# Four weight conversions in another order, in the first slots of an MLP that follows a spectral mixer

## The chip, the cores and the metric

The kernel runs on one core of one Trainium2 chip. The metric is the device time of one execution in microseconds, lower is better; the time before is 2548.9 us, the median of 3 runs (2548.44 to 2549.2).

## What is computed

Eight sequences of 3072 tokens with 256 channels go through a real Fourier transform along the sequence, a complex 256 x 256 mixing with a soft threshold, the inverse transform, and then a two-layer MLP with softplus:

```
X = rfft(x, axis=1);  Yr = Xr @ w_r - Xi @ w_i + b_r;  Yi = Xr @ w_i + Xi @ w_r + b_i
Y = soft_threshold(Yr, 0.01) + 1j * soft_threshold(Yi, 0.01)
x = irfft(Y).reshape(24576, 256)
h = x @ w_in;  g = max(h, 0) + log1p(exp(-|h|));  out = g @ w_out      # 256 -> 2048 -> 256
```

## The kernel before

**Numbers in two parts.** Every matrix product of the MLP is made of three matmuls (`mm3`, L248 to L251): high part times high part, high times low, low times high. So each weight is kept as a pair of a rounded high part and a low part that holds the rest. The first layer's products are further written as a seven-product scheme (the indices A11 to S4 and B11 to T4), so a first-layer weight tile `w1` holds 7 blocks in 2 parts (128 x 1792 numbers of 4 bytes, 896 KB) and a second-layer tile `w2` holds 128 x 1024 (512 KB).

**Keys and slots.** The MLP's work is a list of keys (batch b, pair of token blocks bp, pair of hidden blocks mp). The first eight keys, called key 0 to key 7 here, use the weights with m2 = 0 to 7 of both layers. Each key takes four slots of the program; key k starts at slot 4k. In a slot, `slot_products` issues 3 or 6 first-layer matmuls (tiles `psc` and `pse`), then come one step of the transform work planned for this slot (such as `s1_four`, eight matmuls), loads planned for it, and last `slot_second` issues 6 second-layer matmuls (tile `pso`). Key k reads its `w2` from its own last slot, 4k + 3, to slot 4k + 6, the third of the next key.

**Where weights come from.** In the first pass over the weights the inputs (64-bit numbers) must first be converted. `split_w` (L183 to L238) does that in pieces, one piece a slot: squares and scalings on ScalarE (ACT) and VectorE (DVE), one product on GpSimd (POOL, L203), sums on DVE (L219 to L231 for `w_in`, one L223 for `w_out`), the rounding to the high part on ACT (L233), the low part on DVE (L235), and a store of both parts to DRAM (L237, `w_dr`). Key 0 to key 7 are converted once; a conversion marked `own` in the table `turns` writes straight into a `w1` or `w2` tile which its key then reads, the others write elsewhere and their key loads the tile back from DRAM in `stream_w` (L245): `w1` four slots before its key starts, `w2` one slot before.

```
    def w2_tile():
        return sb.tile([P, 2 * 2 * D], F32R, tag="w2", name="w2")
...
        if own:
            w = w_t[which, (0, 0, m2)] = w1_tile() if which else w2_tile()
...
            for which, lead in ((1, 4), (0, 1)):
                if i >= NM // 2 or (which, i) not in made:
                    at(4 * i - lead, stream_w, which, i % (NM // 2), key)
```

There are two `w1` buffers and two `w2` buffers (the pool has bufs=2). Tiles get them in the order in which the program asks; a tile that asks while both are taken gets the one whose reader is done first, and its first writer waits for that reader. A conversion asks for its own tile in its third piece, two slots after it starts.

**The table.** A row of `turns` is (layer: 1 for w_in, 0 for w_out; m2; slot at which the conversion starts; slot at which the raw weight is loaded; where the raw weight lies; own or not). Loads and stores nearly all stand in one queue, that of SyncE (SP), in the order in which the program issues them; a DMA whose buffer isn't free holds up all that stand behind it there.

Of the kernel before, what the change touches and what calls it, by code (L numbers as in the profile page):

```python
# [34 lines left out]
def tile_spectral_mixer_mlp(ctx, tc, x, w_r, w_i, bias, bias_0, w_in, w_out, f, f_hi, f_lo, g1, g3, g3_hi, g3_lo, hm, out):  # L35
# [77 lines left out]
    def less(src, hi, lo, eng=None, sign=1.0, what=None):  # L113
# [15 lines left out]
        (0, 2, -21, -27, 'l', 0),  # L129
        (1, 4, -16, -22, 'dp', 0),  # L130
        (1, 0, -11, -17, 'w64', 1),
        (1, 5, 3, -3, 2048, 0),
        (0, 3, 7, -2, 3072, 1),
        (1, 6, 9, 1, 4096, 0),
        (0, 4, 12, 6, 0, 1),
        (0, 5, 16, 10, 1024, 1),
        (0, 6, 20, 11, 'w64', 1),
        (1, 7, 22, 12, 'w64', 1),
# [1019 lines left out]
```

## Time and profile before

| | |
|---|---|
| median of 3 runs | 2548.9 us |
| profiled execution | 2550.98 us |
| its span, first to last instruction | 2549.2 us |
| mean granted clock of TensorE in it | 0.994 |
| busy share of the span: PE, DVE, ACT, POOL | 98%, 63%, 64%, 3% |

The profiled execution is 2.1 us above the median of the runs, so a sum made against it is carried over to the median as a difference. PE is TensorE's matmuls, PEld its weight loads. The times in rows are microseconds from the span's start; the four conversions lie between about 134 us (slot 4) and 180 us.

### The profile page before, as it was taken

To read this page: it belongs to the slowest core of one execution; us is meant where nothing else is said; L and a number is where in the kernel's file an instruction comes from. 1 tells how busy PE (TensorE), PEld (TensorE's weight loads), DVE (VectorE), ACT (ScalarE), POOL (GpSimd) and SP (SyncE) were. 2 spreads that over 40 slices of the span, in tenths; PEclk is the share of its full clock that TensorE was granted. 3 is DMA by queue.
4 is the path that set the end of the run, shared out by engine and by line. 5 is a ranking of instruction groups with operands and counts; after the bars stand their busy time and mean duration, and the time that the engine had idled before them with its cause. 6 is when DMAs were issued, how large, how long until landed. Compare 5 with 4: busy or idle time off the path is not lost.

```text
span 2549.2 us, 46550 instructions
## 1 busy us (share of the span) xinstructions
PE 2509.3 (98%) x18092; PEld 2003.1 (79%) x18092; DVE 1608.9 (63%) x2657; ACT 1633.9 (64%) x3005; POOL 63.7 (3%) x127
## 2 busy tenths in 40 slices
PE   8899999999999999999999999999999999999999
PEld 5667778877787777877788777787778887888887
DVE  4688675675665766657656676466664666655554
ACT  4476566666666666666666666666666666666665
POOL 2310000000000000000000000000000000000000
PEclk9899999999999999999999999999999999999999
DMA  8776666657557576575665666666656556455543
GB/s 238 234 235 199 202 205 174 201 179 234 174 168 230 170 214 187 163 222 187 190 204 175 186 203 186 197 186 203 203 181 193 174 174 207 155 160 183 176 153 116
DMA packets 224920, 485.52 MB, mean 190 GB/s; under 512 B 42028, under 2 KB 134796, under 8 KB 224700
## 3 DMA queue, kind: packets, MB, share of 16 engines
q1 hardware_dynamic: 220244, 478.16, 60.5%
q8 instruction: 143, 2.34, 0.4%
q0 software_dynamic: 2624, 2.32, 0.4%
q10 hardware_dynamic: 1832, 2.07, 0.3%
q14 instruction: 77, 0.63, 0.1%
HBM read 373.36 MB, written 82.71 MB: 179 GB/s over the span
## 4 chain that ended last, share of the span: by engine, by line
PE 93%; DMA 3%; DVE 2%; SPq 1%; issue 1%; ACT 1%; POOL 0%; DVEq 0%; ACTq 0%
PE pso L249 15%; PE pso L250 13%; PE pso L251 13%; PE psc L249 7%; PE psc L251 7%; PE psc L250 7%; PE pse L249 5%; PE pse L250 5%; PE pse L251 5%; PE psf L649 3%; PE psf L251 2%; PE psf L250 2%; PE psf L249 2%; PE psf L339 2%; PE psf L594 2%; PE psf L419 2%
## 5 line engine op out<-in xcount | busy, mean ns | idle before, releaser
L794 DVE TENSOR_TENSOR gl<-t,gh 128x512 fp32r<-128x512 f32 x768 | 531.2, 692 | 295.1 <-ACT gh L788 293.0
L773 ACT COPY t<-psc 128x512 f32<-128x512 f32 x576 | 337.2, 585 | 566.8 <-PE psc L251 566.4
L778 DVE TENSOR_TENSOR t<-pse,t 128x512 f32<-128x512 f32 x576 | 396.6, 689 | 423.1 <-ACT t L773 286.1
L249 PE MATMUL pso<-gh,w 128*128 128x512 f32 x1536 | 619.8, 404 | 0.0
L251 PE MATMUL pso<-gh,w 128*128 128x512 f32 x1536 | 599.8, 390 | 0.0
L250 PE MATMUL pso<-gl,w 128*128 128x512 f32 x1536 | 599.7, 390 | 0.0
L788 ACT CAST gh<-t 128x512 fp32r<-128x512 f32 x768 | 476.8, 621 | 78.9 <-PE pso L251 56.6
L784 ACT ACTIVATE t<-t 128x512 f32<-128x512 f32 x576 | 365.4, 634 | 77.1 <-DVE t L778 76.9
L249 PEld LDWEIGHTS pso<-gh,w 128*128 128x128 f32 x1536 | 288.7, 188 | 127.9 <-issue 72.6
L251 PEld LDWEIGHTS pso<-gh,w 128*128 128x128 f32 x1536 | 288.5, 188 | 62.4
L250 PEld LDWEIGHTS pso<-gl,w 128*128 128x128 f32 x1536 | 289.1, 188 | 50.9
L249 PE MATMUL psc<-y_sb,w 128*128 128x512 f32 x768 | 301.4, 392 | 4.0 <-ACT t L773 3.1
L251 PE MATMUL psc<-y_sb,w 128*128 128x512 f32 x768 | 300.0, 391 | 0.0
L250 PE MATMUL psc<-y_sb,w 128*128 128x512 f32 x768 | 299.6, 390 | 0.0
L249 PE MATMUL pse<-y_sb,w 128*128 128x512 f32 x576 | 227.4, 395 | 2.9 <-DVE t L778 2.4
L250 PE MATMUL pse<-y_sb,w 128*128 128x512 f32 x576 | 225.3, 391 | 0.5 <-DVE y_sb L720 0.5
L251 PE MATMUL pse<-y_sb,w 128*128 128x512 f32 x576 | 224.7, 390 | 0.0
L249 PEld LDWEIGHTS psc<-y_sb,w 128*128 128x128 f32 x768 | 144.6, 188 | 37.9 <-ACT t L773 4.0
L251 PEld LDWEIGHTS psc<-y_sb,w 128*128 128x128 f32 x768 | 144.6, 188 | 31.0
L250 PEld LDWEIGHTS psc<-y_sb,w 128*128 128x128 f32 x768 | 144.5, 188 | 29.9
L251 PE MATMUL psf<-wmh,l 128*128 128x256 f32 x504 | 142.6, 283 | 0.0
L250 PE MATMUL psf<-wml,l 128*128 128x256 f32 x504 | 142.5, 283 | 0.0
(159 smaller groups left out, 2809.9 us busy)
## 6 DMA issues: line engine op xcount, KB each, us to landing
w<-w_dr SPq DMA_DIRECT2D x190, 896.0 KB
w<-w_dr SPq DMA_DIRECT2D x185, 512.0 KB
dp<-d_dr SPq DMA_DIRECT2D x114, 192.0 KB
ap<-a_dr SPq DMA_DIRECT2D x168, 128.0 KB
shrunk<-z SPq DMA_DIRECT2D x336, 64.0 KB
d_dr<-d SPq DMA_DIRECT2D x84, 256.0 KB
x<-in_x SPq DMA_DIRECT2D x105, 192.0 KB
a_dr<-a SPq DMA_DIRECT2D x102, 192.0 KB
```

The lines of the kernel that those rows point to most:

```text
L249: nc.tensor.matmul(ps, wh, xh, start=start, stop=False, skip_group_check=more)
L250: nc.tensor.matmul(ps, wh, xl, start=False, stop=False, skip_group_check=more)
L251: nc.tensor.matmul(ps, wl, xh, start=False, stop=stop, skip_group_check=more)
L339: nc.tensor.matmul(banks[i][64 * odd:64 * odd + 64, :], f2[64 * i:64 * i + 48, 64 * odd:64 * odd + 64], t[64 * i:64 * i + 48], start=True, ...
L419: nc.tensor.matmul(xv[n:n + 64, i, v, g, k], t[rows, 2 * i + g, k * P + n:k * P + n + 64], g1_t[rows, 2 * i + g].rearrange("p (c s) -> p c ...
L594: nc.tensor.matmul(banks[e][cols, c], g3_half[rows, kind], both[j][rows, c], start=True, stop=True)
L649: nc.tensor.matmul(banks[v][j:j + m, at:at + n], d[64 * v:64 * v + rows, n2 % 4, k * P + j:k * P + j + m], h[64 * v:64 * v + rows, n2 % 4, ...
L773: nc.scalar.copy(t, banks[bank])
L778: nc.vector.tensor_tensor(out=t, in0=banks[bank], in1=t, op=ALU.add)
L784: nc.scalar.activation(t, banks[bank] if bank else t, AF.Softplus)
L788: nc.scalar.copy(gh, ct[key, what])
L794: nc.vector.tensor_tensor(out=gl, in0=ct.pop((key, what)), in1=gh.bitcast(F32), op=ALU.subtract)
```

## The change

Four rows of the table are written in another order and at other slots. The conversions for key 3 and key 4 of the second layer (`own`) now start at slots 3 and 10 (before 7 and 12), those for key 5 and key 6 of the first layer, which go through DRAM, at 7 and 13 (before 3 and 9). The slots of their raw loads are exchanged with them; the place of each raw weight stays its own.

```
-        (1, 5, 3, -3, 2048, 0),
-        (0, 3, 7, -2, 3072, 1),
-        (1, 6, 9, 1, 4096, 0),
-        (0, 4, 12, 6, 0, 1),
+        (0, 3, 3, -3, 3072, 1),
+        (1, 5, 7, -2, 2048, 0),
+        (0, 4, 10, 1, 0, 1),
+        (1, 6, 13, 6, 4096, 0),
```

No instruction is added or taken away; all that follows is their order. Two places are shown. The first is SP's queue of DMAs from the load of key 2's `w2` on (slot 7). Here `w2_dr2` to `w2_dr4` and `w1_dr3` to `w1_dr6` are the converted weights of key 2 to key 6 in DRAM, `x0` a piece of the next sequence, `a` a result of the first transform step, `stage` the mixing weights, and the number in a tile's name rises with the order in which tiles are asked for. Before:

```order
L245 DMA w2_1260<-w2_dr2_89 128x1024
L237 DMA w1_dr5_84<-y1_78 128x1792
L1038 DMA g3_half_73<-in_g3_hi 128x128
L245 DMA w1_1301<-w1_dr3_82 128x1792
L104 DMA a_dr_189<-a_1296 96x512
L104 DMA a_dr_189<-a_1298 96x512
L318 DMA x0_95<-in_x 48x2x512 x2
L179 DMA y1_78<-in_w_out 128x2x512
L145 DMA stage_1352<-in_w_r 128x2x256
L145 DMA stage_1354<-in_w_i 128x2x256
L179 DMA w64_1388<-in_w_out 128x2x512
L237 DMA w2_dr3_90<-w2_1323 128x1024
```

And with the change:

```order
L245 DMA w2_1255<-w2_dr2_89 128x1024
L237 DMA w2_dr3_90<-w2_1204 128x1024
L1038 DMA g3_half_73<-in_g3_hi 128x128
L245 DMA w1_1296<-w1_dr3_82 128x1792
L104 DMA a_dr_189<-a_1291 96x512
L104 DMA a_dr_189<-a_1293 96x512
L318 DMA x0_95<-in_x 48x2x512 x2
L179 DMA y1_78<-in_w_out 128x2x512
L145 DMA stage_1349<-in_w_r 128x2x256
L145 DMA stage_1351<-in_w_i 128x2x256
L179 DMA w64_1381<-in_w_out 128x2x512
L237 DMA w1_dr5_84<-y1_78 128x1792
```

The places in the queue are the same; the two stores `w1_dr5` and `w2_dr3` have changed places. In both, the bias (256 KB), the raw `w_in` of key 7 (512 KB) and the load of key 4's `w1` (896 KB) come next. The tile of key 3 (`w2_1323` before, `w2_1204` now) was asked for after that of key 2 (`w2_1260`), and is now asked for ahead of it (`w2_1255`).

The second place is ACT's queue around the rounding of an own tile. Before, in slots 9 to 11, key 3's tile (`t` are results of the first layer taken out of the accumulator `psc`, which the next first-layer product overwrites):

```order
L196 ACTIVATE wu_1326<-y1_78 128x512
L199 ACTIVATE y1_78<-y1_78 128x512
L773 COPY t_1344<-psc_1268 128x512
L233 CAST w2_1323<-y1_78 128x512
L784 ACTIVATE t_1344<-t_1344 128x512
```

With the change, in slots 13 to 15, key 4's tile:

```order
L773 COPY t_1443<-psc_1389 128x512
L233 CAST w2_1408<-y1_78 128x512
L196 ACTIVATE wu_1449<-y1_78 128x512
L199 ACTIVATE y1_78<-y1_78 128x512
L773 COPY t_1465<-psc_1389 128x512
```

The rounding now stands ahead of a copy out of the accumulator, with two instructions of the next conversion between them.

## Rows read from the trace of the kernel before

**Rows 1.** The page, part 1: busy time and share of each engine.

```profile
PE 2509.3 (98%) x18092; PEld 2003.1 (79%) x18092; DVE 1608.9 (63%) x2657; ACT 1633.9 (64%) x3005; POOL 63.7 (3%) x127
```

**Rows 2.** Waits of PE from 260 us on: total us, times, longest.

```profile
PE psf L419 <- issue: 1.3, 2, 0.9
PE psc L249 <- DMA w<-w_dr: 0.9, 1, 0.9
```

**Rows 3.** Timeline of PE, slots 10 to 16: start, us, instruction, [idle before, releaser].

```profile
154.87 0.39 PE L251 MATMUL pso<-gh,w 128*128 128x512 f32 x1
...
156.67 0.40 PE L249 MATMUL pso<-gh,w 128*128 128x512 f32 x1
...
158.05 0.39 PE L249 MATMUL psc<-y_sb,w 128*128 128x512 f32 x1
...
160.46 0.50 PE L249 MATMUL pse<-y_sb,w 128*128 128x512 f32 x1 [1.57 <-DVE t L778]
...
167.61 0.50 PE L249 MATMUL psc<-y_sb,w 128*128 128x512 f32 x1 [0.86 <-ACT t L773]
...
172.69 0.39 PE L249 MATMUL psc<-y_sb,w 128*128 128x512 f32 x1
...
173.99 0.50 PE L249 MATMUL pse<-y_sb,w 128*128 128x512 f32 x1 [0.46 <-DVE t L778]
```

**Rows 4.** Timeline of SP's queue, 140 to 164 us: start and length of issue.

```profile
140.00 0.44 SPq L179 DMA_DIRECT2D y<-in_w_out  x1
143.83 0.35 SPq L245 DMA_DIRECT2D w<-w_dr  x1
147.77 0.34 SPq L237 DMA_DIRECT2D w_dr<-y  x1
...
163.50 0.41 SPq L245 DMA_DIRECT2D w<-w_dr  x1
```

**Rows 5.** Chain of waits from 148 us on: start, us, what.

```profile
163.50 6.50 DMA w<-w_dr
```

**Rows 6.** Windows: us, engines' busy time, PE clock, DMA share, GB/s (last two).

```profile
146.00:146.50 0.50, 0.50 (x4) 0.42 (x3) 0.50 (x2) 0.50 (x2) 0.00 (x0) 1.00 1.02 418
146.50:147.00 0.50, 0.50 (x4) 0.42 (x3) 0.50 (x2) 0.50 (x2) 0.00 (x0) 1.00 0.12 41
148.50:153.00 4.50, 4.50 (x22) 3.46 (x19) 3.70 (x7) 4.44 (x9) 1.23 (x1) 1.00 0.98 324
```

**Rows 7.** DMA traffic from 148 to 170 us.

```profile
DMA packets 2853, 6.89 MB, mean 313 GB/s; under 512 B 259, under 2 KB 899, under 8 KB 2851
...
q1 hardware_dynamic: 2851, 6.87, 95.9%
```

**Rows 8.** Timeline of ACT, slots 9 to 11.

```profile
151.87 0.67 ACT L196 ACTIVATE wu<-y 128x512 f32<-128x512 f32 x1
152.44 0.67 ACT L199 ACTIVATE y<-y 128x512 f32<-128x512 uint32 x1
...
155.30 0.62 ACT L233 CAST w<-y 128x512 fp32r<-128x512 f32 x1 [0.77 <-PE pso L251]
155.85 0.63 ACT L784 ACTIVATE t<-t 128x512 f32<-128x512 f32 x1
```

**Rows 9.** Timeline of PE, three of its waits ahead of 134 us.

```profile
28.64 2.34 PE L393 MATMUL psf<-y,ap 128*128 128x128 f32 x8 [2.55 <-ACT y L307]
...
64.97 1.25 PE L393 MATMUL psf<-y,ap 128*128 128x128 f32 x8 [3.19 <-DMA ap<-a]
...
130.45 0.61 PE L249 MATMUL psc<-y_sb,w 128*128 128x512 f32 x1 [2.25 <-ACT t L773]
```

**Rows 10.** Windows after waits of 2.25 and 1.57 us, as in rows 6.

```profile
130.50:134.00 3.50, 3.50 (x9) 2.74 (x10) 3.44 (x7) 2.67 (x5) 0.00 (x0) 0.53 0.02 5
160.50:164.00 3.50, 3.50 (x18) 2.02 (x19) 3.43 (x11) 2.36 (x4) 0.00 (x0) 1.00 0.90 302
```

**Rows 11.** Timeline of PE, its longest wait after 180 us.

```profile
206.35 1.13 PE L393 MATMUL psf<-ap 128*128 128x128 f32 x8 [1.44 <-issue]
```

## The prediction

> **What bounds the kernel now.** I read the page's engine shares first: PE is busy 98% of the span [rows 1]. Next the waits of PE from 260 us to the end: under 2.5 us in nearly 2300 us [rows 2]. So from 260 us on the matmuls follow each other without a gap; what the start loses or gains arrives at the end undiminished, and nothing late takes it up. The change sits between 134 and 180 us, so I read that stretch by engine.
>
> PE's timeline there [rows 3] shows slot 10's last second-layer matmul (the last reader of key 1's `w2`) at 154.87 + 0.39 = 155.26, slot 11's first `pso` matmul (key 2's first read of its `w2`) at 156.67, slot 12 (key 3's first read of its `w1`) at 158.05 and slot 16 (key 4's `w1`) at 172.69. Three waits lie in it: 1.57, 0.86 and 0.46 us.
>
> SP's queue [rows 4] shows where these weights come from. It issues a raw load at 140.00, then stands until key 0's last second-layer matmul frees a buffer, and issues key 2's `w2` at 143.83. From 147.77 on it sends the train shown in the order above, which ends with key 4's `w1`, issued at 163.50. The chain of waits has that load landing at 163.50 + 6.50 = 170.00 [rows 5], 2.7 us ahead of slot 16. Between 148 and 170 us the DMA queue is 95.9% busy at 313 GB/s [rows 7]: this stretch is full. A queue with so little slack must start on time.
>
> **The change, part by part.**
>
> *Work removed or added:* none. The same four conversions run, so DVE, ACT and POOL have the same sum. Key 4's conversion leaves slots 12 to 16 and key 6's enters 13 to 18; I put that at nothing, because PE will be waiting for a DMA then (below). If that cover were gone, it would be a wait of the size seen now, up to 1.57 us.
>
> *Whose buffer key 2's load gets.* Key 3's conversion now starts at slot 3, so it asks for its `w2` tile at slot 5, ahead of key 2's load at slot 7. It takes the buffer of key 0, free after slot 6. Key 2's load gets the buffer of key 1, which is read until the end of slot 10, one slot before key 2 itself is needed. Its issue moves from 143.83 to 155.3, just after 155.26. SP is in order, so everything behind it waits too: the train that began at 147.77 begins at 155.3, with 512 KB of key 2's `w2` in front.
>
> *First wait (slot 11).* Alone in the queue, the 512 KB load issued at 143.83 was moving until the first tenth of the window 146.50 to 147.00 [rows 6], so it took about 2.7 us. Now it lands at 155.3 + 2.7 = 158.0 where PE wants it at 156.67: 1.3 us of waiting. Six matmuls later (158.05 - 156.67 = 1.4 us) PE wants key 3's `w1`, at 159.4.
>
> *Second wait (slot 12).* Ahead of and with key 3's `w1` stand 512 + 64 + 896 KB = 1.51 MB. At the 324 GB/s of the train's first 4.5 us [rows 6] that is 4.65 us; at the 418 GB/s of a quiet moment [rows 6] 3.6. I take 4.2, since the first transfers are large ones: slot 12 starts at 162.2, after 2.8 us of waiting, 4.15 us later than now.
>
> *Third wait (slot 15).* Key 4's own tile now takes the buffer of key 2, read to the end of slot 14. Its rounding on ACT stands ahead of the copy that empties `psc`, and so holds slot 15. On ACT the rounding starts 0.04 us after PE's release and the next instruction 0.55 us later; L196 to L199 is 0.57 us apart [rows 8]. Rounding, L196, L199 and the copy: 0.04 + 0.55 + 0.57 + 0.57 + 0.6 for the copy (about the rounding's 0.62) = 2.3 us. PE's own path from slot 12 to 16 is 172.69 - 158.05 = 14.64, less the waits 1.57 and 0.86 (DVE has time to catch up at slot 12), 12.2 us. With the 2.3 it would be at slot 16 at 162.2 + 12.2 + 2.3 = 176.7.
>
> *Fourth wait (slot 16).* Key 4's `w1` ends the train. By the sizes in the order above (896 + 64 + 896 + 4 x 192 + 512 + 512 + 512 + 512 + 256 + 512 + 896 KB) the train is 6336 KB, 6.49 MB, the same set before and after. Two ways to time it: at 313 GB/s it takes 20.7 us, landing at 158.0 + 20.7 = 178.7; or as it was timed, 170.00 - 147.77 = 22.2 us from first issue, less about 0.7 until data moved, 158.0 + 21.5 = 179.5. I take the middle, 179.1. It is later than PE's 176.7, so the transfer sets slot 16, and the second and third waits are hidden in it. Slot 16 starts 179.1 - 172.69 = 6.4 us late. Its wait of 0.46 for DVE goes, DVE having long finished.
>
> *After slot 16* the next load, key 5's `w1`, has 1.8 MB ahead of and with it and lands some 6 us after 179.1, at 185; PE needs it four slots (12 us) later. The train is caught up, and the rest keeps its distance to PE.
>
> **Sum:** +6.4 - 0.46 = +5.9, taken as 6.0 us. Against the profiled execution's own time that is 2550.98 + 6.0 = 2557.0; against the median of the runs, 2548.9 + 6.0 = **2554.9 us**. A measurement of this kernel can tell about 0.2%, 5.1 us, from no change; the forecast lies just beyond that.
>
> **The clock.** After PE's waits of 2.25, 2.55 and 3.19 us [rows 9] TensorE ran at half clock for a time (0.53 granted, mostly 1.2 GHz, from 130.5 to 134.0), but after 1.57 us it stayed at 2.4 GHz [rows 10]. In those 3.5 us 9 matmuls came; at full clock six take 1.38 us [rows 3], so 9 would take 2.1, a loss of 1.4 us. I expect it after the second wait, 2.8 us. There it costs nothing: PE arrives at slot 16 at 178.1 instead of 176.7, still before 179.1. The Trainium skill, TensorE: Matmul & The Clock Gate, section Part 1: The HAM clock gate, has the half rate as the default state that activity lifts; the rows above agree for waits over 2 us. By it the sum would grow by another 1.4 us if the gate closes at slot 16 as well.
>
> **The rivals.**
>
> 1. *Clock paid at slot 16.* If the clock holds after slot 12, PE waits 2.4 us at slot 16 and may lose it there, uncovered: 6.0 + 1.4 = +7.4, 2556.3 us. For it: the three waits of about this size [rows 9] did so, though not every one before 134 us. Against it: the earlier wait of 2.8 us should come first. Chance 0.16.
>
> 2. *The queue drains faster.* If it ran at the 418 GB/s that a quiet half microsecond shows [rows 6], 6.49 MB would take 15.5 us and key 4's `w1` would be there at 173.5. Then PE's own 176.7 decides: 176.7 - 172.69 - 0.46 = +3.6, 2552.5 us. Against it: engines 95.9% busy at 313 GB/s [rows 7] with the same transfers. The Trainium skill, Perfetto Trace Analysis, section Roofline, puts the 16 DMA engines of a core at about 435 GB/s together. By it the train would take 14.9 us and the sum would be +3.6 too; this stretch shows 313. Chance 0.12.
>
> 3. *Taken up later.* PE's longest wait after 180 us is 1.44 us, at 206 [rows 11]. If it were set by something that doesn't move with PE, 6.0 shrinks to +4.6, 2553.5 us. Against it: PE's work feeds what it waits for. Chance 0.07.
>
> 4. *Key 2's load isn't held (faster).* If the tile asked for first doesn't take key 0's buffer, key 2's load still goes out at the end of slot 6, at about 143.8, and the train keeps its time. What is left is a lighter DVE at slots 11 and 12, where key 6's seven sums now stand later: the waits 1.57, 0.86 and 0.46 could go, -2.9, 2546.0 us. It decides at one point: whether SP issues the load ahead of or after 155 us. For it only that the order doesn't show a buffer's release; against it, two buffers and the order of the tiles. Here the change wouldn't do what its order says. Chance 0.07.
>
> **How the numbers follow.** The forecast has 0.58. Of it I count 0.53 as slower by over 0.2%, since its own range (slot 16 set by a landing between 178.7 and 180.2) is +5.5 to +7, and a landing at 178 would fall short. With rival 1 that makes slower 0.69; rivals 2 and 3 and the rest of the forecast are within 0.2%, 0.24; rival 4 is faster by 0.11%, and only with more waits gone by over 0.2%, so I leave 0.05 for that and 0.26 for within. The range has to hold the forecast, rival 1 with 2 us more of the same, and rivals 2 and 3: 2552.0 to 2558.7; rival 4 and unseen waits stay outside.
>
> **What would show it.** Right: SP stands from about 140.5 to 155.3 ahead of key 2's `w2`, with the DMA queue idle for most of it; PE waits for `w<-w_dr` in slots 11, 12 and 16; slot 15's `psc` waits for ACT; slot 16 starts near 179; from 190 us on every row is about 6 us later. Wrong: SP issues that load near 144; or no wait for a weight at slot 16; or slot 16 late by 6 us but the shift gone by 240 us.

## The result, and the profile after

| | before | after |
|---|---|---|
| median of 4 runs, us | 2548.67 (2547.81 to 2549.2) | 2562.14 (2560.14 to 2566.24) |
| ratio, 95% interval | | 1.0056 (1.0044 to 1.0068) |
| profiled execution: its time, its span, us | 2550.98, 2549.2 | 2562.65, 2560.9 |

The change is slower by 13.5 us, where 6.0 were forecast. A second timing, beside the last experiments, gave a ratio of 1.0041 (1.0028 to 1.0054).

The page's engine shares of the changed kernel hold the same instructions as [rows 1] and 9.4 us more of busy PE, which is matmuls that took longer:

```profile
PE 2518.7 (98%) x18092; PEld 2004.8 (78%) x18092; DVE 1609.9 (63%) x2657; ACT 1634.5 (64%) x3005; POOL 63.9 (2%) x127
```

SP's queue in the changed kernel (start, length of issue), against [rows 4]:

```profile
136.98 0.43 SPq L179 DMA_DIRECT2D y<-in_w_in  x1
152.38 0.35 SPq L245 DMA_DIRECT2D w<-w_dr  x1
...
164.12 0.33 SPq L245 DMA_DIRECT2D w<-w_dr  x1
...
177.43 0.34 SPq L237 DMA_DIRECT2D w_dr<-w  x1
```

Key 2's `w2`, which went out 11.4 us ahead of the end of slot 10's last matmul before (143.83 against 155.26), now goes out at that end (151.96 + 0.39 = 152.35; issued at 152.38). For 15 us SP issues nothing.

PE's timeline of the changed kernel, against [rows 3]: slot 10's last reader, then the waits up to 200 us and the starts of slot 16 (180.54) and of one matmul near 260 us of before (the last row):

```profile
151.96 0.39 PE L251 MATMUL pso<-gh,w 128*128 128x512 f32 x1
...
156.53 0.80 PE L249 MATMUL pso<-gh,w 128*128 128x512 f32 x1 [2.66 <-DMA w<-w_dr]
...
160.93 0.77 PE L249 MATMUL psc<-y_sb,w 128*128 128x512 f32 x1 [1.47 <-DMA w<-w_dr]
...
176.09 0.72 PE L249 MATMUL psc<-y_sb,w 128*128 128x512 f32 x1 [2.28 <-ACT t L773]
...
180.54 0.39 PE L249 MATMUL psc<-y_sb,w 128*128 128x512 f32 x1
...
185.97 0.50 PE L249 MATMUL pse<-y_sb,w 128*128 128x512 f32 x1 [0.32 <-DVE t L778]
...
189.50 0.50 PE L249 MATMUL psc<-y_sb,w 128*128 128x512 f32 x1 [1.19 <-ACT t L773]
...
196.36 0.50 PE L249 MATMUL pse<-y_sb,w 128*128 128x512 f32 x1 [0.94 <-DVE t L778]
...
270.56 0.66 PE L594 MATMUL psf<-shrunk,g_half 64*64 64x512 f32 x4
```

The matmul of the last row starts at 260.10 before. So the stretch from slot 10's last matmul to it took 260.10 - 154.87 = 105.2 us before and 270.56 - 151.96 = 118.6 now: **+13.4 us**, about the 13.5 of the medians. This length is the measure in every experiment below. It leaves out what comes earlier, and that matters: slot 10's end itself fell anywhere between 4.4 us earlier and 0.9 later than in the first profile of before (2.9 earlier in the changed kernel, which is why the two profiled executions differ by 11.7 us only). The half-clock stretches ahead of slot 4 also lie elsewhere in each profile; what moves slot 10's end was not followed. The length itself repeats well: run 5 below, in which nothing came out otherwise than before, ended slot 10 1.7 us earlier and has the length of before, 105.2.

The windows of the changed kernel (columns as in [rows 6]) show the idle queue, the half clock after the two waits, the end of the train, and the half clock after slot 15's wait:

```profile
141.00:152.00 11.00, 11.00 (x52) 7.98 (x52) 10.00 (x20) 8.66 (x16) 1.30 (x1) 1.00 0.01 3
155.80:169.30 13.50, 11.30 (x29) 6.81 (x30) 6.86 (x11) 4.78 (x9) 1.52 (x1) 0.50 1.04 352
...
174.00:174.50 0.50, 0.00 (x0) 0.00 (x0) 0.00 (x0) 0.50 (x2) 0.00 (x0) 1.00 0.54 207
174.50:175.00 0.50, 0.00 (x0) 0.00 (x0) 0.00 (x0) 0.50 (x2) 0.00 (x0) 1.00 0.21 82
...
176.20:179.60 3.40, 3.40 (x9) 2.66 (x10) 3.37 (x6) 2.74 (x5) 0.95 (x1) 0.50 0.38 154
```

The train was through at about 174.5, 6 us ahead of slot 16, which shows no wait for its weight. On ACT, slot 15's wait reads as forecast: rounding, L196, L199 and then the copy (against [rows 8]):

```profile
173.85 0.62 ACT L233 CAST w<-y 128x512 fp32r<-128x512 f32 x1 [3.52 <-PE pso L251]
174.37 0.65 ACT L196 ACTIVATE wu<-y 128x512 f32<-128x512 f32 x1
174.93 0.63 ACT L199 ACTIVATE y<-y 128x512 f32<-128x512 uint32 x1
175.47 0.56 ACT L773 COPY t<-psc 128x512 f32<-128x512 f32 x1
```

The account by waits of PE in this stretch (150 to 260 us; total, times, longest), before and then after:

```profile
PE pse L249 <- DVE t L778: 2.4, 3, 1.6
PE psf L393 <- issue: 1.4, 1, 1.4
PE psc L249 <- ACT t L773: 0.9, 1, 0.9
PE psf L649 <- DVE sum L480: 0.7, 1, 0.7
```

```profile
PE psc L249 <- ACT t L773: 3.5, 2, 2.3
PE pso L249 <- DMA w<-w_dr: 2.7, 1, 2.7
PE pse L249 <- DVE t L778: 1.7, 3, 0.9
PE psc L249 <- DMA w<-w_dr: 1.5, 1, 1.5
PE psf L393 <- issue: 1.0, 1, 1.0
PE psf L649 <- DVE sum L480: 0.7, 1, 0.7
```

These are 5.4 us before and 11.1 after: 5.7 of the 13.4. The other 7.7 lie in no wait. PE was busy for 11.30 us and 3.40 us at half clock. A matmul follows every 0.43 us there (166.27, 166.69, 167.12) and every 0.23 us at full clock (six in 1.38 us, [rows 3]), so these two stretches cost about 6.8 us; 0.9 us stay unassigned.

### The profile page after: what moved, and what is told of

It reads as the page before. It is cut to its first block, busy times and chain, and to the rows that moved or that the text cites. A ratio compares the mean times of both kernels' runs of the same rounds, so it can differ in the third digit from the quotient of the medians.

```text
span 2560.9 us, 46545 instructions
## 1 busy us (share of the span) xinstructions
PE 2518.7 (98%) x18092; PEld 2004.8 (78%) x18092; DVE 1609.9 (63%) x2657; ACT 1634.5 (64%) x3005; POOL 63.9 (2%) x127
## 4 chain that ended last, share of the span: by engine, by line
PE 92%; DVE 3%; DMA 3%; issue 1%; ACT 1%; SPq 1%; POOL 0%; DVEq 0%; POOLq 0%; ACTq 0%
PE pso L249 15%; PE pso L251 13%; PE pso L250 13%; PE psc L249 7%; PE psc L251 7%; PE psc L250 7%; PE pse L249 5%; PE pse L250 5%; PE pse L251 5%; PE psf L649 3%; PE psf L251 2%; PE psf L250 2%; PE psf L249 2%; PE psf L339 2%; PE psf L594 2%; PE psf L419 2%
```

## The experiments

Theory 1: the cost is the hold of key 2's `w2` load. Theory 2: it is the second half of the change, keys 4 and 6. Theory 3: about half of it is the half clock after the waits, and the waits alone are the rest. "Shift" is the length defined above less 105.2, from one profile each; "half clock" is how long TensorE was granted 0.5 between slot 10 and 200 us; the ratio is that of the timed runs, each against the kernel before on the same chip.

| run | shift, us | half clock, us | ratio (95%) |
|---|---|---|---|
| the change, first profile | +13.4 | 13.7 + 3.4 | 1.0056 (1.0044 to 1.0068) |
| the change, second profile (11) | +11.2 | 3.4 | 1.0041 (1.0028 to 1.0054) |
| 1 first half | +11.2 | 6.8 + 3.4 | 1.0051 (1.0036 to 1.0066) |
| 2 second half | +4.6 | 0 | 1.0013 (1.0004 to 1.0022) |
| 3 through DRAM (order without hold) | +4.4 | 3.4 | 1.0026 (1.0015 to 1.0038) |
| 4 filled | +10.1 | 0 | 1.0040 (1.0026 to 1.0055) |
| 5 asked for early | 0.0 | 0 | 0.9996 (0.9986 to 1.0005) |
| 6 key 4 back at 12 | +8.8 | 3.4 | 1.0041 (1.0028 to 1.0055) |
| 7 key 6 alone to 13 | +2.0 | 0 | 1.0000 (0.9991 to 1.0009) |
| 8 key 4 alone to 10 | +3.4 | 6.8 | 1.0015 (1.0005 to 1.0025) |
| 9 written early (hold alone) | +6.2 | 3.4 + 6.8 | 1.0019 (1.0010 to 1.0029) |
| 10 key 6 alone to 11 | +0.4 | 0 | 0.9999 (0.9989 to 1.0009) |
| 12 key 6 to 11, key 4 to 13 | +1.5 | 0 | 1.0002 (0.9993 to 1.0011) |

**Run 1.** In the order of before:

```diff
-        (1, 5, 3, -3, 2048, 0),
-        (0, 3, 7, -2, 3072, 1),
+        (0, 3, 3, -3, 3072, 1),
+        (1, 5, 7, -2, 2048, 0),
```

> Keys 3 and 5 are exchanged as in the change (slots 3 and 7); keys 6 and 4 stay at 9 and 12 as before. Theory 1 (the cost comes from key 2's w2 load being held until the end of slot 10): waits of PE for w of about 2.7 and 1.5 us in slots 11 and 12, half clock after them, no wait of 2.3 us for ACT in slot 15; +6 to +10 us against before. Theory 2 (the cost comes from keys 4 and 6, slots 15 to 19): within 2 us of before. Theory 3 (about half of the cost is the half clock after the waits) expects some 10 to 14 us of half clock after slot 11, against 0 to 4 in the kernel before.

Waits of 1.51 and 2.83 us for `w` in slots 11 and 12 are there, but so is one of 4.08 for ACT in slot 14, which no theory had. ACT's timeline names it:

```profile
169.10 0.94 ACT L233 CAST y<-y 128x896 fp32r<-128x896 f32 x1 [6.76 <-DMA w_dr<-y]
```

Keys 5 and 6, two slots apart here, share the one tile of their conversions, and key 6's rounding waits for the store of key 5's (key 6's sums fall into key 5's unfinished tile, so key 5's weights are not computed here). The run has a wait of its own making and does not measure the first half; run 9 does.

**Run 2.** In the order of before:

```diff
-        (1, 6, 9, 1, 4096, 0),
-        (0, 4, 12, 6, 0, 1),
+        (0, 4, 10, 1, 0, 1),
+        (1, 6, 13, 6, 4096, 0),
```

> Keys 5 and 3 stay at slots 3 and 7 as before; keys 4 and 6 are exchanged and moved to 10 and 13 as in the change. Key 2's load should go out at about 143.8 us as before. Theory 1: no wait for w in slots 11 and 12; the wait for ACT of 2.3 us in slot 15, a short half clock after it (loss 1.7 us) and the waits of about 1 us at slots 18 and 19 stay: +2 to +6 us. Theory 2: +10 us or more.

There is no wait for `w`, and key 2's load goes out at 142.24, 11.0 us ahead of slot 10's last matmul as before. PE's timeline from slot 12 to 20:

```profile
157.17 0.50 PE L249 MATMUL psc<-y_sb,w 128*128 128x512 f32 x1 [0.79 <-ACT t L784]
168.62 0.50 PE L249 MATMUL psc<-y_sb,w 128*128 128x512 f32 x1 [2.28 <-ACT t L773]
173.93 0.50 PE L249 MATMUL pse<-y_sb,w 128*128 128x512 f32 x1 [1.57 <-DVE t L778]
178.48 0.50 PE L249 MATMUL pse<-y_sb,w 128*128 128x512 f32 x1 [0.28 <-DVE t L778]
182.00 0.50 PE L249 MATMUL psc<-y_sb,w 128*128 128x512 f32 x1 [1.16 <-ACT t L773]
188.86 0.50 PE L249 MATMUL pse<-y_sb,w 128*128 128x512 f32 x1 [0.94 <-DVE t L778]
```

These are 7.0 us of waits in place of the 2.9 of before: +4.1 of the +4.6. So the second half by itself is about a third of the cost, not the whole of it and not nothing.

**Run 3.** In the changed kernel, key 3's `w2` is converted into another buffer and read back:

```diff
-        (0, 3, 3, -3, 3072, 1),
+        (0, 3, 3, -3, 3072, 0),
```

> The change with its order of conversions whole, but key 3's converted w2 goes into a buffer of its own and comes back through memory like those of the other keys (one more 512 KB load, asked for at slot 11), so it asks for no w2 tile at slot 5 and key 2's load gets key 0's buffer. Theory 1: SP sends key 2's load near 144 us, the waits in slots 11 and 12 go, slot 15's wait for ACT stays: +2 to +6 us, the same as with the second half alone. Theory 2: +10 us or more. If the order of the conversions itself costs the time (whatever the buffer): +13 us.

SP's queue, then PE's timeline:

```profile
142.17 0.35 SPq L245 DMA_DIRECT2D w<-w_dr  x1
```

```profile
168.37 0.50 PE L249 MATMUL psc<-y_sb,w 128*128 128x512 f32 x1 [2.28 <-ACT t L773]
```

The waits for `w` are gone, and key 2's load goes out early. The shift, +4.4, is near that of run 2, so the order of keys 3 and 5 by itself shows no cost in this length. The ratios leave one open: 1.0026 here against 1.0013, with intervals that overlap; this run also has one load of 512 KB more, and 3.4 us at half clock where run 2 has none.

**Run 4.** Added matmuls in the changed kernel:

```diff
+        def fill_pe(n):
+            ps = psf()
+            for _ in range(n):
+                nc.tensor.matmul(ps, wmh[:, 0, 0, :P], tokens((0, 0), B11)[0], start=True, stop=True)
...
+            if i == 11:
+                fill_pe(11)
...
+            if i in (11, 14):
+                fill_pe(12 if i == 11 else 10)
```

> The change, with added matmuls that nobody reads and that wait for nothing: 11 ahead of slot 11's second layer, 12 at its end, 10 at the end of slot 14's products, 33 x 0.23 = 7.6 us of PE time at 2.4 GHz, placed where PE would stand for 2.7, 3 and 2.3 us. All waits and their causes stay, only PE is kept at work. Theory 3 (the half clock after the waits costs some 7 us): no half clock after slot 10, and +5 to +8 us against before in place of the change's +13.5. Rival (the clock costs nothing, the waits and the late transfers set the time): +13 us or more.

There is no half clock after slot 10; the shift is +10.1, between the two numbers. By slot 16 PE was 4.8 us ahead of the first profile of the change (a shift of +5.9 there against +10.8). But slot 16 then waited 1.55 us for DVE, a wait that the slower PE of the first profile did not meet:

```profile
180.68 0.50 PE L249 MATMUL pse<-y_sb,w 128*128 128x512 f32 x1 [1.55 <-DVE t L778]
```

So Theory 3 holds in kind and not in size: against that execution filling returned 3.3 us, not 7. Against the change's second profile, which had 3.4 us at half clock, it returned 1.0. The ratio, 1.0040, is not clear of either timing of the change, so in time the gain is not shown.

**Run 5.** In the kernel before:

```diff
-            w = w_t[which, (0, 0, m2)] = w1_tile() if which else w2_tile()
+            w = w_t[which, (0, 0, m2)] = asked.pop((which, m2), None) or (w1_tile() if which else w2_tile())
...
+        at(5, lambda: asked.update({(0, 3): w2_tile()}))
```

> The kernel before with its order of conversions untouched; only the w2 tile of key 3 is asked for at slot 5 (its conversion still starts at slot 7), so key 2's load gets key 1's buffer and waits for the end of slot 10. This is the hold by itself. Theory 1 (the buffer order is the cause): no SP issue between about 140 and 152 to 155 us, PE waits for w in slots 11 and 12 of 2 to 3 us each, half clock after them, +8 to +12 us. Theory 2 or 'the order of the conversions costs': within 2 us of before. As no conversion moves, slot 15 should wait for ACT no longer than the 0.86 us of before.

This was a miss: nothing changed, and key 2's load went out as early as before (slot 10's last matmul is at 153.17 here):

```profile
142.13 0.35 SPq L245 DMA_DIRECT2D w<-w_dr  x1
```

So asking for the tile takes no buffer, and the sentence ahead of the prediction that tiles get their buffers in the order in which the program asks is wrong. That left the hold unproved, and run 9 was made for it.

**Run 6.** In the changed kernel, key 4 back at 12:

```diff
-        (0, 4, 10, 1, 0, 1),
-        (1, 6, 13, 6, 4096, 0),
+        (0, 4, 12, 6, 0, 1),
+        (1, 6, 13, 1, 4096, 0),
```

> Key 3 at slot 3 and key 5 at 7 as in the change, key 4 back at 12 as before, key 6 at 13 with its raw load at slot 1. Compared with the change only key 4 is two slots later. If the holds in slots 11 and 12 carry the time: +9 to +13 us. If slot 15's wait of 2.3 us for ACT came from key 4 at slot 10 it should now be about 0.9 us and the time some 2 us less than the change's, +11 us; if it came from the tile of key 2 that key 4 waits for, whatever its slot, it stays.

PE waits for `w` for 2.70 and 2.81 us. Slot 15 has no wait at all: key 4's rounding now comes after slot 15's copies and waits for nothing itself (slot 16 starts at 176.32, after 0.19 us):

```profile
176.10 0.61 ACT L233 CAST w<-y 128x512 fp32r<-128x512 f32 x1
```

So slot 15's wait comes from key 4 at slot 10. The shift is 2.4 us less than that of the change's second profile; the ratio is the same, 1.0041, so in time no gain is shown.

**Runs 7 and 8.** In the order of before, one key moved in each:

```diff
-        (1, 6, 9, 1, 4096, 0),
+        (1, 6, 13, 1, 4096, 0),
```

```diff
-        (0, 4, 12, 6, 0, 1),
+        (0, 4, 10, 1, 0, 1),
```

> The order of before, with key 6 alone moved from slot 9 to 13. Key 2's load goes out near 144 us; no wait for w. If key 6's seven sums on DVE make the waits of 1.57, 0.86 and 0.46 us at slots 12, 15 and 16, those shrink, and the time is between 3 us less and equal to before; if key 6 at 13 causes the waits at slots 18 and 19 (1.2 and 0.9 us) these appear here too, and the sum is -1 to +2 us. Theory 2 (the second half costs 10 us) expects +5 us or more.

> The order of before, with key 4 alone moved from slot 12 to 10 (raw load at slot 1). If key 4 at slot 10 makes the 2.3 us wait for ACT in slot 15, it shows here: +1 to +3 us; if that wait comes with key 6 at 13, slot 15 waits 0.9 us as before and the time is within 1 us.

(The wait of 0.86 us, at 167.61 before, which these expectations put in slot 15, lies in slot 14; slot 15 starts at 169.80.) Key 6 at 13 takes the waits of 1.57 and 0.86 us away (PE is 3.0 us ahead at slot 14) and gives 5 us back in slots 15 to 20. Key 4 at 10 costs 3.4 us, and most of that is half clock: it came with a wait of 1.78 us for DVE in slot 12, and all waits together grew by only 0.7 us (0.58, 1.78 and 1.19 in place of 2.9):

```profile
160.60:167.40 6.80, 6.24 (x18) 3.31 (x19) 6.70 (x15) 4.33 (x7) 1.53 (x1) 0.50 0.80 238
```

Slot 15 waits 1.19 us for ACT here, not 2.3; why less was not tried. The two shifts, 2.0 + 3.4, add up to near run 2's 4.6, but not from the same parts, as run 2 had no half clock.

**Run 9.** As run 5, with the tile also written early:

```diff
+        def write_early():
+            asked[0, 3] = w2_tile()
+            nc.gpsimd.memset(asked[0, 3][:, :8].bitcast(F32), 0.0)
...
+        at(6, write_early)
```

> As in the run with the tile asked for early, but GpSimd also writes zeros into 8 columns of the tile at slot 6 (they are overwritten by the conversion), since that run showed that asking alone takes no buffer. All conversions stay in the order of before. Theory 1 (whoever writes first takes key 0's buffer, and key 2's load then waits for the end of slot 10): SP stands from about 140 to 152 or later, PE waits for w of 2 to 3 us in slots 11 and 12, half clock after them, +7 to +12 us. Theory 'the order of the conversions, not the buffer, costs the time': within 2 us of before, with key 2's load again near 143 us.

No conversion was moved to another slot, and the hold is there. SP's queue, then PE's timeline:

```profile
135.63 0.42 SPq L179 DMA_DIRECT2D y<-in_w_out  x1
150.92 0.35 SPq L245 DMA_DIRECT2D w<-w_dr  x1
```

```profile
155.07 0.80 PE L249 MATMUL pso<-gh,w 128*128 128x512 f32 x1 [2.62 <-DMA w<-w_dr]
...
160.51 0.47 PE L249 MATMUL psc<-y_sb,w 128*128 128x512 f32 x1 [2.51 <-DMA w<-w_dr]
```

+6.2 us for the hold by itself, with 10.2 us at half clock. The two waits, 5.1 us, take the place of the 2.9 of before; the other 4 us are the slower matmuls. With the +4.4 of the order without the hold (run 3) that is 10.6, against 11.2 in the change's second profile; in the timed ratios 4.8 and 6.6 us, 11.4, between the change's 10.5 and 14.3. So both theories have a part, and the two parts make about the whole. Which is the larger is not shown: the shifts say the hold, the ratios the order, and the intervals of the ratios overlap. That the shifts add up is partly luck, too: runs 9 and 3 together have 4.6 us of added waits and 13.6 us at half clock, the second profile 8.9 and 3.4 (run 11).

**Runs 10 and 12**, searches for a version that beats both, with key 6 at 11 in the order of before, and key 4 at 12 or 13:

> The order of before with key 6 moved from slot 9 to 11, a search for a version that beats both. Moving it to 13 took away the waits of 1.57 and 0.86 us at slots 12 and 15 but brought others of 1.2 and 0.9 us at slots 18 and 19. If two slots are enough for the first and too few for the second: -1 to -2.5 us between slot 10 and 260 us. Otherwise within 1.5 us of before.

> The order of before with key 6 at slot 11 (as in the last search) and key 4 one slot later, at 13. With key 6 at 11 and key 4 at 12 PE was 2.75 us ahead of before up to slot 15 and lost it to one wait of 2.6 us for DVE in that slot. If key 4's two steps on DVE and GpSimd stood in that wait, moving them one slot on takes most of it away: -1.5 to -2.5 us between slot 10 and 260 us, which in time is within what a measurement can tell. If key 6's seven sums alone make it, it stays and the shift is within 1 us of 0.

Neither does. Both are 2.8 to 3.0 us ahead at slot 14 and lose it to DVE in slots 15 and 16 (2.61, or 1.91 and 0.95 us). Nothing that was run beats the kernel before.

**Run 11.** The changed kernel again:

> The changed kernel once more, beside the kernel before on the same chip. If the half clock after the waits in slots 11 and 12 lasts as long as in the first profile (13.65 us), the shift between slot 10 and 260 us is again +13 us; if its length differs between executions (the runs with the same waits had 3.4 to 6.8 us), it is +9 to +11 us. In time: +10 to +14 us.

PE's timeline of this second profile:

```profile
160.52 0.50 PE L249 MATMUL pso<-gh,w 128*128 128x512 f32 x1 [2.80 <-DMA w<-w_dr]
164.91 0.47 PE L249 MATMUL psc<-y_sb,w 128*128 128x512 f32 x1 [2.73 <-DMA w<-w_dr]
177.72 0.50 PE L249 MATMUL psc<-y_sb,w 128*128 128x512 f32 x1 [2.28 <-ACT t L773]
...
180.61 0.39 PE L249 MATMUL psc<-y_sb,w 128*128 128x512 f32 x1
...
183.02 0.50 PE L249 MATMUL pse<-y_sb,w 128*128 128x512 f32 x1 [1.57 <-DVE t L778]
187.57 0.50 PE L249 MATMUL pse<-y_sb,w 128*128 128x512 f32 x1 [0.30 <-DVE t L778]
191.10 0.50 PE L249 MATMUL psc<-y_sb,w 128*128 128x512 f32 x1 [1.16 <-ACT t L773]
```

With only 3.4 us at half clock the shift is +11.2, and the six waits plus one of 0.93 at 197.95 are 11.8 us against 2.9 before. So the waits are 8.9 of it, and the length of the half clock, with the waits that it moves, is what differs between executions of the change.

## Why the prediction was wrong

*The hold: right.* Key 2's load waits for the end of slot 10 because key 3's own tile takes key 0's buffer. What was wrong is how: not by asking first (run 5) but by writing first (run 9); in the change key 3's rounding, at slot 6, writes ahead of the load at slot 7.

*First wait, mis-sized:* 2.66 and 2.80 us against 1.3. The 512 KB took 4.1 to 4.3 us from issue to first reader (152.38 to 156.53; 156.20 to 160.52), not the 2.7 of a load alone in the queue: the stores and loads that SP held back follow it at once (0.88 MB had moved between 152 and 156.5 us, not 0.52).

*Second wait: right* in size, 2.73 us against 2.8, in the second profile, where the clock was still full; 1.47 in the first, where PE came to it at half clock.

*Third wait: right* in size, 2.28 us against 2.3, and it was paid, where the forecast hid it.

*Fourth wait: the step that failed.* "... the transfer sets slot 16" was the forecast, at 179.1, 23.8 us after the hold's end. The queue was through 22.1 us after it in the first profile (152.38 to about 174.5), since the train moved faster than the 313 GB/s that were assumed (352 from 155.8 to 169.3 us), while PE needed 24.4 (156.20 to 180.61) in the second, and 28.2 in the first. PE decided, as in rival 2. PE's own path had been put at 176.7 - 155.3 = 21.4; of the 3.0 us more in the second profile 1.6 are the first load, 0.2 the second wait's end, and 1.2 lie in slots 12 to 16 (180.61 - 164.91 = 15.7 against 14.5), where the half clock was. So slot 16 was late by 7.0 us (172.69 - 154.87 = 17.8 from slot 10's last matmul before, 180.61 - 155.78 = 24.8 now), close to the forecast's 6.4 by luck, for another reason.

*"Work removed or added ... I put that at nothing, because PE will be waiting for a DMA then": the second half of the same failure.* With no transfer to wait for, the cover was gone. From slot 16 on the second profile loses 11.2 - 7.0 = 4.2 us more, most of it in waits of 1.57, 0.30, 1.16 and 0.93 us for ACT and DVE, where key 6's conversion now stands; before there is one of 0.46, and the sum took that off. The price named for the lost cover, one wait of up to 1.57 us, was too small: it came as four.

*The clock, "There it costs nothing", because hidden by the transfer:* not hidden. It cost about 7 us in the first profile by its busy time, and 3.3 us as what filling it returned against that profile (1.0 against the second). Rival 1 had the cost in kind, 1.4 us, for a clock that stayed down 3.5 us [rows 10]; it stayed down 3.4 us in one execution and 13.7 in another. The range was built on one fall of 3.5 us.

*"... nothing late takes it up": right*, with an addition. From 260 us to the end the difference grew, by 1.2 and 4.2 us in the two profiles of the change, 4.8 in run 3, and 2.0 or less in the others. PE's waits from 260 us on, for `w` and at L419, and in the second profile a half-clock stretch of 3.4 us at 1463, go with it; why they differ was not tried.

So the cost is the hold, 6.2 us with the half clock that it brought in run 9 (4.8 in the timed runs), and the order without it, keys 4 and 6 at 10 and 13, 4.4 us in run 3 (6.6 in the timed runs); the further 2.2 us of the first profile go with its longer half clock. How the half clock's length comes about stays open, and with it the exact split.

## What to carry to other kernels

When a term is costed at nothing because something later hides it, compute both finish times with their errors: here 2.4 us (179.1 against 176.7) separated cover from no cover, while the forecast was off by 1.7 us on the queue and by 3.0 us on PE's path. In a pool of rotating buffers look for who writes first, not who asks first: one early conversion took the free buffer from a load, and the in-order queue stood still behind that load for 15 us. And where PE is 98% busy, a conversion moved from one crowded stretch to another moves its waits with it: five other arrangements of keys 4 and 6 (runs 2, 7, 8, 10 and 12) gave no gain.

## What the runs showed of the hardware

- *The half clock can outlast the wait by far while PE is busy.* From 162 to 168 us of the first profile PE was busy for 6.00 of 6.00 us and the granted clock was 0.50 throughout. After two waits for the same two loads it stayed down 13.7 us (first profile), 3.4 (second, run 6) and 3.4 + 6.8 in two pieces (run 9). The Trainium skill, TensorE: Matmul & The Clock Gate, section Part 1: The HAM clock gate, has the half rate as a state that activity lifts; the trace agrees that it is lifted in the end, and how long that took could not be told ahead from the waits.

```profile
162.00:168.00 6.00, 6.00 (x19) 3.06 (x18) 3.18 (x5) 3.33 (x6) 0.00 (x0) 0.50 1.07 343
```

- *The length of a wait does not tell whether it comes.* The wait of 2.28 us in slot 15 brought it in the first profile and in run 3, and not in the second profile, nor in run 2. With 1.78 us it came in run 8, with 2.61 us it did not in run 10.
- *The held-back train moved faster than the same train on time:* 352 GB/s over 13.5 us and 333 over the whole 22.1 us from 152.4 on, against 313 over 22 us before [rows 7]. What made it faster is not shown.
